# Taking a hand-written scheduler's operations by longest remaining path, and letting PSUM copies choose their engine

## The chip, the core and the metric

The kernel runs on one core of a Trainium2 chip. A core has five instruction streams that work side by side: TensorE (PE in the profile; its weight loads are PEld), VectorE (DVE), ScalarE (ACT), GpSimd (POOL) and SyncE (SP, which here only issues transfers). TensorE writes its products into PSUM, eight banks of 128 partitions by 512 fp32 values; VectorE and ScalarE read them there. The streams wait for each other by semaphores. The metric is the device time of one execution in microseconds, and the median over several runs is compared.

## What is computed

Two layers, each of a linear attention and a gated block, over x of 2048 rows by 512 columns in bf16. The attention has 32 heads of 16 columns. Cut to what matters:

```python
def _A_ref(x, wqkv, w_phi, wo):
    q, k, v = split_heads(x @ wqkv)
    pq, pk = q @ w_phi, k @ w_phi          # per head
    phi_q = concat(softmax(pq), softmax(-pq))
    phi_k = concat(softmax(pk), softmax(-pk))
    kv = phi_k.T @ v                       # summed over all 2048 rows
    z = phi_k.sum(rows)
    o = (phi_q @ kv) / (phi_q @ z + 1e-6)
    return merge_heads(o) @ wo

def _B_ref(x, W_gate, W_up, W_down):       # 512 -> 1376 -> 512
    return (relu(x @ W_gate) * (x @ W_up)) @ W_down

for _ in range(2):
    x = x + _A_ref(_layernorm(x), ...)
    x = x + _B_ref(_layernorm(x), ...)
```

`kv` and `z` need the keys of all rows before the first query can be answered. That is the one barrier in each layer.

## The kernel before

**Scheduler.** The kernel describes itself as a list of `Op` objects and plans its own order while it is built. Each `Op` (line 43) has an engine, a function that emits the instruction, what it reads and writes, and two durations in ns: `occ`, how long it holds its engine, and `lat`, when its result is there. `Program.op` (69) and `Program.dma` (74) append them in program order. `derive` (79) turns reads and writes into dependences. A buffer that is used in turn gives a dependence of the next writer on the last readers, so rings of buffers tie the program's parts together; between two products into the same PSUM bank only the order is kept. `schedule` (117) is a list scheduler: it repeatedly looks at all operations whose predecessors are placed, works out for each the earliest start on its engine, and takes the one with the smallest pair of start and `prio`. `prio` is the index in the program (line 55). So an operation that can start now goes ahead of a more important one that must wait, and among those that can start at the same time the one that stands earlier in the program goes first. A PSUM bank is given out when the first product that writes it is placed, and comes back when its last reader is done. Signals between engines cost 120 ns and within an engine 60 ns in the plan (59 and 60). `plan` (184) then places the semaphore waits, and `emit` (221) writes each engine's operations in the planned order. On the chip each engine goes through its own list in that order, whatever happens.

**Work.** The 2048 rows are 4 blocks (`st`) of 4 tiles (`t`) of 128 rows. x stays in SBUF throughout.

- `fold` (382) multiplies the key and query weights by the per-head `w_phi` once, at the start.
- `layernorm(st)` (401): for each of four tiles `bn_stats` and `bn_aggr` on VectorE; then the reciprocal square root of the four variances together, in twelve small VectorE steps, each waiting for the one before (415 to 423); then for each tile the apply into `ytile` (429; four buffers), four TensorE transposes, and a copy out of PSUM into `yT` (437 to 441): odd tiles on VectorE, even ones on ScalarE.
- `keys(st, b)` (447): for each tile the key and value products, two exponentials on ScalarE into `expk` (six buffers), the sums `Zk` (466; two buffers) and their reciprocals `rZk` on VectorE, a copy of the values into `vsb` on ScalarE (three buffers), and two GpSimd products `vhat` (475). For the block: the `kv` products and a copy or addition into `kvsum` (488, 491) on VectorE.
- `sums()` (494): the barrier. Eight pairs of VectorE steps make `ZDw` (500) and `kvbd` (503) from `kvsum`.
- `queries(st, b)` (507): 16 products and 8 exponentials on ScalarE into `expq`.
- `attend(st)` (516): 32 narrow products `zd`; a chain on VectorE (a copy `Zs` at 530, then `zm`, `zden`, the reciprocal `zr` and `atok`); transposes of `atok` and the copy `aT` (542); then, for each of four column groups, two products that spread `aT` over the partitions, two VectorE products into `expq` (547), the numerator products, and a copy `oT` on ScalarE (552); at last the products with `wo` and the residual additions (561).
- `glu(st, b)` (563): for each of 11 column groups four gate and four up products, a relu on ScalarE (576; `gate_sb` has three buffers) and a product on VectorE into `hT` (578; 22 buffers); then for each tile 11 down products into one bank, and a residual.

**Order.** In the program (602 to 617) the four blocks' layernorms and keys come first. Then, in each layer: `sums`; `out_of_a(0)` (queries, attention and layernorm of block 0); and for each block `st`: `out_of_a(st + 1)`, `glu(st)`, and then `into_a(st)` (the next layer's layernorm and keys) in layer 1, or the four stores of the block in layer 2. Every store writes the one name `R("out")`, so each store depends on the store before it.

Of the kernel before, what the change touches and what calls it, by code (L numbers as in the profile page):

```python
# [42 lines left out]
class Op:  # L43
    __slots__ = ("idx", "eng", "fn", "reads", "writes", "occ", "lat", "name", "is_dma", "nbytes",
                 "deps", "odeps", "users", "missing", "ready", "start", "finish", "cnt", "stream", "prio")

    def __init__(self, idx, eng, fn, reads, writes, occ, lat, name, is_dma=False, nbytes=0):
        self.idx, self.eng, self.fn = idx, eng, fn
        self.reads, self.writes = list(reads), list(writes)
        self.occ, self.lat, self.name = float(occ), float(lat), name  # L50
        self.is_dma, self.nbytes = is_dma, nbytes
        self.deps, self.odeps, self.users = set(), set(), []
        self.missing, self.ready = 0, 0.0
        self.start = self.finish = self.cnt = self.stream = None
        self.prio = idx


class Program:
    SYNC = 120.0
    SAME = 60.0  # L60
# [12 lines left out]

    def dma(self, eng, fn, reads=(), writes=(), nbytes=0, name=""):
        o = Op(len(self.ops), eng, fn, reads, writes, self.DMA_ISSUE[eng], 0, name, True, nbytes)
        self.ops.append(o)
        return o

# [37 lines left out]

    def schedule(self):
        self.derive()
        free = {e: 0.0 for e in ENGINES}
# [3 lines left out]
        left = len(self.ops)  # L123
        for o in self.ops:
            if not o.missing:
                ready[o.eng].append(o)
# [4 lines left out]
        while left:  # L131
            best = None
            for e in ENGINES:
                for o in ready[e]:
                    s = max(free[e], o.ready)
# [7 lines left out]
                    key = (s, o.prio)  # L143
                    if best is None or key < best[:2]:
                        best = (s, o.prio, o)
            assert best is not None, "no operation can go on"
            s, _, o = best
            ready[o.eng].remove(o)
# [10 lines left out]
            o.start = s  # L159
            if o.is_dma:  # L160
                free[o.eng] = s + o.occ
# [3 lines left out]
            else:  # L165
                free[o.eng] = s + o.occ
                o.finish = s + o.lat
            for r in set(o.reads) | set(o.writes):
                if isinstance(r, Bank):
                    r.left -= 1  # L170
                    if not r.left:
                        t = max(x.finish + (0.0 if x.eng == "pe" else self.SYNC) for x in r.ops)
                        banks.append((t, r.bank, r))
            for u in o.users:
                if o.idx in u.deps:
                    t = o.finish + (self.SAME if u.eng == o.eng and not o.is_dma else self.SYNC)
                    u.ready = max(u.ready, t)
                u.missing -= 1
                if not u.missing:
                    ready[u.eng].append(u)  # L180
# [58 lines left out]
def build_kernel(nc, A_x, A_wqkv, A_w_phi, A_wo, W_gate, W_up, W_down, out):  # L239
# [8 lines left out]
    with ExitStack() as ctx:  # L248
# [58 lines left out]
        op, dma = prog.op, prog.dma  # L307
# [4 lines left out]
        def mm(ps, view, lhsT, rhs, start, stop, reads, n, name):  # L312
            lat = 0.4167 * n + 167
            op("pe", lambda e: e.matmul(view(ps), lhsT, rhs, start=start, stop=stop),  # L314
               reads=reads, writes=[ps], occ=max(25.0, 0.4167 * n + 2.6), lat=lat, name=name)

        def tr(ps, view, src, reads, name):
            op("pe", lambda e: e.transpose(view(ps), src, ident[:]),  # L318
               reads=list(reads) + [R("ident")], writes=[ps], occ=56, lat=220, name=name)
# [4 lines left out]
        def b16half(ps):  # L324
            return ps.b16()[:, 0:512]

# [8 lines left out]
        def load_x(t0, t1):  # L335
# [27 lines left out]
           reads=[R("mask8a")], writes=[R("mask8")], occ=150, name="mask8")  # L363
        op("pool", lambda e: e.affine_select(EC[:].rearrange("p g (h j) -> p g h j", j=16), ones[:].rearrange("p (g h j) -> p g h j", g=8, j=16),
                                             [[-8, 8], [-1, 8], [0, 16]], ALU.is_equal, 0.0, base=0, channel_multiplier=1),
# [35 lines left out]
        def layernorm(st):  # L401

            for t in range(4 * st, 4 * st + 4):
                op("dve", (lambda t: lambda e: e.bn_stats(stats[:, t, :], x_sb[:, t, :]))(t), reads=[R("x", t)], writes=[R("st", t)], occ=580, lat=680, name=f"bn{t}")  # L404
                op("dve", (lambda t: lambda e: e.bn_aggr(mv[:, t, :], stats[:, t, :]))(t), reads=[R("st", t)], writes=[R("mv", t)], occ=70, lat=172, name=f"ba{t}")  # L405
            ts = range(4 * st, 4 * st + 4)
            var = mv[:, 4 * st:4 * st + 4, 1:2]
            y = rstd[:, 4 * st:4 * st + 4, :]
            v, hx, t1 = rsv[:, st], rsh[:, st], rst[:, st]
            Rmv, Ry, Rv, Rh, Rt = [R("mv", t) for t in ts], [R("rs", t) for t in ts], [R("rv", st)], [R("rh", st)], [R("rt", st)]  # L410

            def small(fn, reads, writes):
                op("dve", fn, reads=reads, writes=writes, occ=65, lat=160, name="rstd")

            small(lambda e: e.tensor_scalar(v, var, float(EPS_LN), None, op0=ALU.add), Rmv, Rv)
            small(lambda e: e.tensor_scalar(hx, var, 0.5, 0.5 * float(EPS_LN), op0=ALU.mult, op1=ALU.add), Rmv, Rh)
            small(lambda e: e.tensor_single_scalar(t1.bitcast(I32), v.bitcast(I32), 1, ALU.logical_shift_right), Rv, Rt)
            small(lambda e: e.tensor_scalar(y.bitcast(I32), t1.bitcast(I32), -1, 0x5F3759DF, op0=ALU.mult, op1=ALU.add), Rt, Ry)
            for _ in range(2):
                small(lambda e: e.tensor_tensor(t1, y, y, ALU.mult), Ry, Rt)  # L420
                small(lambda e: e.tensor_tensor(t1, t1, hx, ALU.mult), Rt + Rh, Rt)
                small(lambda e: e.tensor_scalar(t1, t1, -1.0, 1.5, op0=ALU.mult, op1=ALU.add), Rt, Rt)
                small(lambda e: e.tensor_tensor(y, y, t1, ALU.mult), Ry + Rt, Ry)
            b = cnt["yT"] % NYT
            cnt["yT"] += 1
            for t in ts:
                yb = cnt["y"] % NY
                cnt["y"] += 1
# [7 lines left out]
                if tt % 2:  # L436
                    op("dve", (lambda ps, dst: lambda e: e.tensor_copy(dst, b16half(ps).rearrange("p (c n) -> p c n", c=NC)))(ps, dst),
                       reads=[ps], writes=[R("yT", b, tt)], occ=328, lat=415, name=f"ycp{t}")
                else:
                    op("act", (lambda ps, dst: lambda e: e.activation(dst, b16half(ps).rearrange("p (c n) -> p c n", c=NC), ACT.Copy))(ps, dst),  # L440
                       reads=[ps], writes=[R("yT", b, tt)], occ=480, lat=600, name=f"ycp{t}")
# [5 lines left out]
        def keys(st, b):  # L447
# [30 lines left out]
            for g0, g1 in ((0, 3), (3, 6), (6, 8)):  # L478
# [8 lines left out]
                if st == 0:  # L487
                    op("dve", (lambda ps, dst, n: lambda e: e.tensor_copy(dst, ps.f32()[:, 0:n]))(ps, dst, n),  # L488
                       reads=[ps], writes=[R("kvs", g0)], occ=490, lat=580, name="kvs")
# [26 lines left out]
        def attend(st):  # L516
# [13 lines left out]
            op("dve", lambda e: e.tensor_copy(Zs[:, g], zdv(zd)[:, :, 0]), reads=[zd], writes=[R("Zs", g)], occ=330, lat=420, name="Zs")  # L530
# [11 lines left out]
            op("dve", lambda e: e.tensor_copy(aT[:, g, :], b16half(pa)), reads=[pa], writes=[R("aT", g)], occ=328, lat=415, name="aT")  # L542
            for c in range(NC):
# [8 lines left out]
                op("act", (lambda c, pn: lambda e: e.activation(oT[:, g, c, :], full(pn), ACT.Copy))(c, pn), reads=[pn], writes=[R("oT", g, c)], occ=480, lat=610, name=f"oT{st}")  # L552
# [49 lines left out]
        for st in range(NS):  # L602
            into_a(st)
# [71 lines left out]
```

## Time and profile before

| what | value |
|---|---|
| median of 3 runs | 454.07 us (452.1 to 454.61) |
| profiled execution | 453.24 us |
| its span, first to last instruction | 451.5 us |
| mean granted TensorE clock | 0.985 |
| HBM read, written | 8.44 MB, 2.10 MB |

The profile's page gives, for one execution, the busy time of each engine and, in 40 slices of the span (11.3 us each), the busy share in tenths: 9 is 90% or more. A view by stretches gives the same for stretches that are asked for, with the share of full speed that TensorE's clock was granted. A group of instructions shows its number, its total busy time, the mean ns of one, and the engine's idle time just ahead of them with what ended it. The timeline lists instructions in order of time; in square brackets stands the idle time of the engine ahead of one, and what it waited for. All matmuls go through the helper at line 314 and all transposes through that at line 318, so they are told apart by their tiles.

### The profile page before, as it was taken

How to read it: one execution, taken by the hardware profiler on the slowest of the kernel's cores; microseconds unless marked ns; L12 is line 12 of the kernel's file. 1: busy time of each engine (PE TensorE's matmuls, PEld its weight loads, DVE VectorE, ACT ScalarE, POOL GpSimd, SP SyncE). 2: the span in 40 equal slices, each digit the busy share in tenths (PEclk: the TensorE clock that was granted, in tenths of full speed). 3: DMA queues.
4: the chain of work that ended last, by engine and by line, in shares of the span. 5: the costliest groups of instructions: out<-in, count | busy, mean ns of one | idle time of the engine just before them, and what ended most of it. 6: DMA issues, size and time to landing. Idle time of an engine off the chain costs nothing.

```text
span 451.5 us, 6587 instructions
## 1 busy us (share of the span) xinstructions
PE 419.7 (93%) x2512; PEld 211.2 (47%) x2560; DVE 331.3 (73%) x819; ACT 182.0 (40%) x329; POOL 72.9 (16%) x75
## 2 busy tenths in 40 slices
PE   3969899789999999999999999887999999999997
PEld 2545556334544544444445444632454454444443
DVE  5999977999669956997578476799963863883342
ACT  4768687223406440453145249622340340341230
POOL 3335780000000700070007005100000000000000
PEclk9999999979999999999999999988999999999999
DMA  8930000000000000000000000000001001000001
GB/s 260 384 107 1 0 1 2 1 0 1 0 1 2 1 1 0 2 0 1 0 1 1 1 0 1 1 1 1 0 2 46 1 0 37 12 1 23 23 1 46
DMA packets 9567, 10.95 MB, mean 24 GB/s; under 512 B 992, under 2 KB 8512, under 8 KB 9536
## 3 DMA queue, kind: packets, MB, share of 16 engines
q1 hardware_dynamic: 7952, 9.47, 6.1%
q10 hardware_dynamic: 1584, 1.07, 0.8%
q8 instruction: 20, 0.33, 0.3%
q14 instruction: 11, 0.09, 0.1%
HBM read 8.44 MB, written 2.10 MB: 23 GB/s over the span
## 4 chain that ended last, share of the span: by engine, by line
PE 77%; DVE 19%; DMA 1%; issue 1%; ACT 1%; POOL 0%; SPq 0%
PE pb L314 74%; DVE expq L547 4%; PE pb L318 3%; DVE stats L404 3%; DVE x_sb L561 2%; DVE Zk L466 1%; DMA x_sb<-in_A_x_dram 1%; DVE kvsum L491 1%; DVE ytile L429 1%; DVE zr L535 1%; DVE hT L578 1%; DVE kvsum L488 1%; DVE kvbd L503 0%; DVE mv L405 0%; DVE Zs L530 0%
## 5 line engine op out<-in xcount | busy, mean ns | idle before, releaser
L576 ACT ACTIVATE gate_sb<-pb 128x512 bf16<-128x512 f32 (+1 forms) x88 | 52.5, 596 | 138.3 <-PE pb L314 136.0
L475 POOL TENSOR_TENSOR vhat<-vsb,rZk 128x544 bf16<-128x544 bf16 x64 | 68.5, 1102 | 210.6 <-DVE rZk L468 195.4
L578 DVE TENSOR_TENSOR hT<-gate_sb,pb 128x512 bf16<-128x512 bf16 (+1 forms) x88 | 59.8, 680 | 44.0 <-PE pb L314 43.8
L314 PE MATMUL pb<-yT,Wg 128*128 128x512 bf16 (+1 forms) x340 | 91.1, 379 | 0.4
L314 PE MATMUL pb<-yT,Wu 128*128 128x512 bf16 (+1 forms) x345 | 91.1, 379 | 0.3
L314 PE MATMUL pb<-Wd,hT 128*128 128x512 bf16 (+1 forms) x344 | 77.0, 379 | 0.4
L561 DVE TENSOR_TENSOR x_sb<-x_sb,pb 128x512 bf16<-128x512 bf16 x64 | 42.2, 683 | 47.0 <-PE pb L314 47.0
L314 PEld LDWEIGHTS pb<-Wd,hT 128*128 128x128 bf16 (+1 forms) x352 | 34.3, 98 | 41.5
L314 PEld LDWEIGHTS pb<-yT,Wu 128*128 128x128 bf16 (+1 forms) x352 | 34.8, 100 | 37.2
L314 PEld LDWEIGHTS pb<-yT,Wg 128*128 128x128 bf16 (+1 forms) x352 | 34.7, 100 | 36.5
L552 ACT ACTIVATE oT<-pb 128x512 bf16<-128x512 f32 x32 | 18.9, 597 | 68.6 <-PE pb L314 68.5
L404 DVE BATCH_NORM_STATS2 stats<-x_sb 128x6 f32<-128x512 bf16 x64 | 42.6, 675 | 1.0 <-DMA x_sb<-in_A_x_dram 0.5
L466 DVE TENSOR_REDUCE Zk<-expk 128x64 f32<-128x1024 bf16 x32 | 37.9, 1190 | 5.4 <-ACT expk L464 5.3
L547 DVE TENSOR_TENSOR expq<-expq,pb 128x512 bf16<-128x512 bf16 x64 | 41.2, 677 | 0.9 <-PE pb L314 0.9
L513 ACT ACTIVATE expq<-pb 128x512 bf16<-128x512 f32 x64 | 33.0, 623 | 18.9 <-PE pb L314 18.8
L464 ACT ACTIVATE expk<-pb 128x512 bf16<-128x512 f32 x64 | 35.0, 602 | 9.6 <-PE pb L314 6.9
L314 PE MATMUL pb<-wo_sb,oT 128*128 128x512 bf16 x125 | 34.4, 379 | 0.3
L314 PE MATMUL pb<-Wkp,yT 128*128 128x512 bf16 x121 | 32.7, 383 | 0.6 <-issue 0.2
L314 PE MATMUL pb<-wv,yT 128*128 128x512 bf16 x126 | 32.7, 379 | 0.1
L314 PE MATMUL pb<-yT,Wqp 128*128 128x512 bf16 x121 | 30.9, 379 | 0.2
L314 PE MATMUL pb<-aT,EC 128*128 128x512 bf16 x64 | 21.7, 460 | 9.6 <-DVE aT L542 9.5
L314 PE MATMUL pb<-vhat,expk 128*128 128x136 bf16 x256 | 25.0, 223 | 3.3 <-POOL vhat L475 2.9
(59 smaller groups left out, 378.0 us busy)
## 6 DMA issues: line engine op xcount, KB each, us to landing
out_dram<-x_sb SPq DMA_DIRECT2D x16, 128.0 KB, 1.7
x_sb<-in_A_x_dram SPq DMA_DIRECT2D x3, 512.0 KB, 10.0
Wg<-in_B_W_gate_dram SPq DMA_DIRECT2D x1, 1376.0 KB, 11.9
Wu<-in_B_W_up_dram SPq DMA_DIRECT2D x1, 1376.0 KB, 12.9
Wd<-in_B_W_down_dram SPq DMA_DIRECT2D x1, 1280.0 KB, 16.1
hT<-in_A_wqkv_dram ACTq DMA_DIRECT2D x1, 512.0 KB, 5.0
x_sb<-in_A_x_dram SPq DMA_DIRECT2D x2, 256.0 KB, 4.7
wv<-in_A_wqkv_dram ACTq DMA_DIRECT2D x1, 512.0 KB, 8.4
```

The source lines that it names most:

```text
L314: op("pe", lambda e: e.matmul(view(ps), lhsT, rhs, start=start, stop=stop), reads=reads, writes=[ps], occ=max(25.0, 0.4167 * n + 2.6), lat ...
L318: op("pe", lambda e: e.transpose(view(ps), src, ident[:]), reads=list(reads) + [R("ident")], writes=[ps], occ=56, lat=220, name=name)
L404: op("dve", (lambda t: lambda e: e.bn_stats(stats[:, t, :], x_sb[:, t, :]))(t), reads=[R("x", t)], writes=[R("st", t)], occ=580, lat=680, ...
L464: op("act", (lambda i, s, pk: lambda e: e.activation(expk[:, i, s, :], full(pk), ACT.Exp, scale=1.0 - 2.0 * s))(i, s, pk), reads=[pk], wri ...
L466: op("dve", (lambda i, zb: lambda e: e.tensor_reduce(Zk[:, zb, :], expk[:, i, :, :].rearrange("p s (h f) -> p (s h) f", f=16), AX.X, ALU.a ...
L475: op("pool", (lambda i, s, vb, rz: lambda e: e.tensor_tensor(vhat[:, i, s, :, :], vsb[:, vb, :, :], rZk[:, rz, s * 32:(s + 1) * 32].unsque ...
L513: op("act", (lambda c, s, ps: lambda e: e.activation(expq[:, st, c, s, :], full(ps), ACT.Exp, scale=1.0 - 2.0 * s))(c, s, ps), reads=[ps], ...
L547: op("dve", (lambda c, sg, ps: lambda e: e.tensor_tensor(expq[:, st, c, sg, :], expq[:, st, c, sg, :], full(ps), ALU.mult))(c, sg, ps), re ...
L552: op("act", (lambda c, pn: lambda e: e.activation(oT[:, g, c, :], full(pn), ACT.Copy))(c, pn), reads=[pn], writes=[R("oT", g, c)], occ=480 ...
L561: op("dve", lambda e: e.tensor_tensor(x_sb[:, t, :], x_sb[:, t, :], full(ps), ALU.add), reads=[R("x", t), ps], writes=[R("x", t)], occ=590 ...
L576: op("act", (lambda m, gb, pg: lambda e: e.activation(gate_sb[0:m, gb, :], pg.f32()[0:m, :], ACT.Relu))(m, gb, pg), reads=[pg], writes=[R( ...
L578: op("dve", (lambda m, gb, hb, pu: lambda e: e.tensor_tensor(hT[0:m, hb, :], gate_sb[0:m, gb, :], pu.f32()[0:m, :], ALU.mult))(m, gb, hb, pu),
```

## The change

The operations and their arithmetic stay the same, but for one term: the halved variance of the layernorm is made from the variance with the epsilon added (`v`), where it was made from the variance itself. What changes is the order in which the scheduler takes the operations, its table of durations, and the engine of some copies.

- `rank` gives every operation the length of the longest way from it to the end of the program, by the planner's durations; `prio` is its negative, so among operations that can start at the same time the one with the longest way goes first. The program's index only breaks ties.
- `SYNC` becomes a table: signals to TensorE cost 90 ns in the plan, from TensorE none, between VectorE and ScalarE 35 or 92, and so on; the latencies of products and transposes are raised.
- `either` makes an operation that can go to one of two engines. When the scheduler takes it, it goes to the engine on which it ends first.
- `copy` uses it for five copies out of PSUM: `yT` (which was split by odd and even tiles), the first block's `kvsum`, `Zs` and `aT` (which were on VectorE), and `oT` (which was on ScalarE).
- `layernorm` reserves its `ytile` buffers ahead of its operations; the sequence of buffers is the same.

```diff
+    SYNC = {("dve", "dve"): 35.0, ("act", "dve"): 35.0, ("act", "act"): 92.0, ("dve", "act"): 92.0,
+            ("dve", "pool"): 80.0, ("act", "pool"): 80.0, ("pool", "pool"): 150.0}
+    SYNC_TO_PE, SYNC_OF_PE, SYNC_ELSE = 90.0, 0.0, 120.0
...
+    def either(self, ways, reads=(), writes=(), name=""):
+        eng = next(iter(ways))
+        o = self.op(eng, ways[eng][0], reads, writes, ways[eng][1], ways[eng][2], name)
+        o.alts = ways
+        return o
...
+    def rank(self):
+        way = [0.0] * len(self.ops)
+        for o in reversed(self.ops):
+            lat = self.DMA_LAT + o.nbytes / self.DMA_BW if o.is_dma else o.lat
+            for u in o.users:
+                step = lat + self.sync(o.eng, u.eng) if o.idx in u.deps else o.occ
+                way[o.idx] = max(way[o.idx], way[u.idx] + step)
+            o.prio = -way[o.idx]
...
-                    key = (s, o.prio)
-                    if best is None or key < best[:2]:
-                        best = (s, o.prio, o)
+                    key = (s, o.prio, o.idx)
+                    if best is None or key < best[:3]:
+                        best = (s, o.prio, o.idx, o, e)
...
+            if o.alts:
+                s, e = min((max(free[x], t) + o.alts[x][2], x) for x in o.alts for y, t in ready[x] if y is o)
+                o.eng = e
+                o.fn, o.occ, o.lat = o.alts[e]
+                s -= o.lat
...
-            lat = 0.4167 * n + 167
             op("pe", lambda e: e.matmul(view(ps), lhsT, rhs, start=start, stop=stop),
-               reads=reads, writes=[ps], occ=max(25.0, 0.4167 * n + 2.6), lat=lat, name=name)
+               reads=reads, writes=[ps], occ=max(25.0, 0.4167 * n + 2.6), lat=max(300.0, 0.4167 * n + 180) if n > 32 else 420, name=name)
...
+        def copy(ps, dst, view, writes, dve, act, name):
+            either({"dve": (lambda e: e.tensor_copy(dst, view(ps)), dve, dve + 88), "act": (lambda e: e.activation(dst, view(ps), ACT.Copy), act, act + 120)},
+                   reads=[ps], writes=writes, name=name)
...
-            small(lambda e: e.tensor_scalar(hx, var, 0.5, 0.5 * float(EPS_LN), op0=ALU.mult, op1=ALU.add), Rmv, Rh)
+            small(lambda e: e.tensor_scalar(hx, v, 0.5, None, op0=ALU.mult), Rv, Rh)
...
-                if tt % 2:
-                    op("dve", (lambda ps, dst: lambda e: e.tensor_copy(dst, b16half(ps).rearrange("p (c n) -> p c n", c=NC)))(ps, dst),
-                       reads=[ps], writes=[R("yT", b, tt)], occ=328, lat=415, name=f"ycp{t}")
-                else:
-                    op("act", (lambda ps, dst: lambda e: e.activation(dst, b16half(ps).rearrange("p (c n) -> p c n", c=NC), ACT.Copy))(ps, dst),
-                       reads=[ps], writes=[R("yT", b, tt)], occ=480, lat=600, name=f"ycp{t}")
+                copy(ps, dst, lambda p: b16half(p).rearrange("p (c n) -> p c n", c=NC), [R("yT", b, tt)], 328, 480, f"ycp{t}")
...
+                    copy(ps, dst, (lambda n: lambda p: p.f32()[:, 0:n])(n), [R("kvs", g0)], 490, 400, "kvs")
...
+            copy(zd, Zs[:, g], lambda p: zdv(p)[:, :, 0], [R("Zs", g)], 330, 270, "Zs")
...
+            copy(pa, aT[:, g, :], b16half, [R("aT", g)], 328, 480, "aT")
...
+                copy(pn, oT[:, g, c, :], full, [R("oT", g, c)], 590, 480, f"oT{st}")
```

## The prediction

> **What bounds the kernel now.** I read the page first (part 1, then the 40 slices), to see which engine is full and when.
>
> ```profile
> span 451.5 us, 6587 instructions
> ...
> PE 419.7 (93%) x2512; PEld 211.2 (47%) x2560; DVE 331.3 (73%) x819; ACT 182.0 (40%) x329; POOL 72.9 (16%) x75
> ...
> PE   3969899789999999999999999887999999999997
> PEld 2545556334544544444445444632454454444443
> DVE  5999977999669956997578476799963863883342
> ACT  4768687223406440453145249622340340341230
> POOL 3335780000000700070007005100000000000000
> ```
>
> TensorE is the bound. It is idle 451.5 - 419.7 = 31.8 us, and the 9s show that nearly all of that lies in slices 0 to 8, 25 to 27 and 39. No order can beat 419.7 us by much, so the change can only win from those 31.8 us, or add to them. Second view: busy time of each engine by stretch (columns: PE, PEld, DVE, ACT, POOL, granted clock, DMA share, GB/s).
>
> ```profile
> 12.00:34.00 22.00, 18.01 (x140) 10.71 (x140) 21.66 (x66) 15.54 (x30) 8.60 (x8) 1.00 0.68 241
> 34.00:72.00 38.00, 36.17 (x267) 20.55 (x271) 33.46 (x74) 29.97 (x58) 25.72 (x24) 1.00 0.00 1
> 72.00:80.00 8.00, 7.11 (x117) 4.63 (x117) 6.73 (x25) 4.98 (x10) 0.00 (x0) 1.00 0.01 3
> 80.00:90.00 10.00, 7.16 (x59) 3.60 (x58) 10.00 (x23) 2.39 (x4) 0.00 (x0) 0.98 0.01 2
> 90.00:101.00 11.00, 8.94 (x30) 3.34 (x32) 10.59 (x35) 2.39 (x4) 0.00 (x0) 0.70 0.00 0
> ...
> 282.00:292.00 10.00, 8.87 (x149) 6.27 (x150) 6.64 (x29) 7.03 (x14) 2.03 (x2) 1.00 0.01 2
> 292.00:303.00 11.00, 9.97 (x68) 4.75 (x69) 10.71 (x27) 2.39 (x4) 0.00 (x0) 0.84 0.01 1
> 303.00:318.00 15.00, 10.74 (x55) 4.62 (x54) 14.59 (x44) 3.58 (x6) 0.00 (x0) 0.89 0.00 1
> ```
>
> TensorE's idle time is 4.0 us in 12 to 34, 1.8 in 34 to 72, 5.8 in 72 to 101, 6.4 in 282 to 318. (The rest: 7.7 before 12 us, loads and the first layernorm; 2.95 at the end, the last residual and its store; 3 us spread over all else.) In 12 to 34, 80 to 101 and 292 to 318 VectorE is 96 to 100% busy: these are the start, and the first attention of each layer, when no gated block is ready to fill TensorE. Third view, the timeline there:
>
> ```profile
> 86.80 0.61 PE L318 MATMUL pb<-ident,atok 128*128 128x128 bf16 x8
> ...
> 91.30 0.39 DVE L542 COPY aT<-pb 128x512 bf16<-128x512 bf16 x1
> ...
> 91.75 3.17 PE L314 MATMUL pb<-aT,EC 128*128 128x512 bf16 x7 [4.34 <-DVE aT L542]
> ```
>
> The copy of aT is ready at 87.4 and runs at 91.3, behind residuals and bn_stats on VectorE, while ScalarE is idle. Last, the groups that price the two homes of a copy:
>
> ```profile
> L440 ACT ACTIVATE yT<-pb 128x512 bf16<-128x512 bf16 x32 | 18.7, 607 | 13.8 <-PE pb L318 13.4
> L437 DVE COPY yT<-pb 128x512 bf16<-128x512 bf16 x32 | 12.6, 413 | 1.5 <-PE pb L318 1.5
> ```
>
> **The change part by part**, against the profiled execution: 453.24 us, a span of 451.5 and 1.74 around it; it lies 0.83 under the median of 454.07.
>
> (a) *Start.* The second layernorm has its first bn_stats at 12.48 and its apply at 32.39. Its own work is 4 bn_stats at 0.59 apart, 4 bn_aggr, 12 small steps 0.2 apart and 1.4 of apply: 6.5 us. The rest are Zk reductions (1.19 each) and rZk (0.54) of the first key tiles, which stand earlier in the program, and bn_stats of later blocks. TensorE starves meanwhile, and GpSimd waits 11.3 us for the next vsb. By the new rank the layernorm goes first: Zk has two buffers, so the planner's chain Zk, rZk, Zk is (1200+35+534+35)/2 = 0.90 us a tile, 14.4 us for sixteen; tile 4's layernorm has twelve tiles of that behind it (10.8) plus its own steps and its keys (some 6.5), 17 us. But rank only chooses between operations that are ready. The small steps stand 195 ns apart in the planner and hold VectorE for 70, so another operation still slips into each gap: 12 x 0.58 = 7 us instead of 13.4 - 2.4 = 11. With the two Zk before it also gone (19.0 becomes 16), the apply comes near 16 + 2.4 + 7 = 25.4 to 28, some 4 to 7 us earlier. TensorE can gain no more than it idles in 12 to 72, 5.8 us, and VectorE's total is unchanged. I take **-3**; bounds -5.8 and +2 (Zk late, so that GpSimd, 16 x 2.15 = 34.4 us, ends last).
>
> (b) *sums().* The eight ZDw steps now go before the eight kvbd (0.2 apart), which only the later num products need. The last ZDw starts at 72.25, with six kvbd between it and the last kvsum: 6 x 0.2 = 1.2 us, while VectorE then waits 1.20 us for the zd products, where the kvbd now fit. **-1 in each layer, -2**; bounds -2.4 and 0.
>
> (c) *Copies.* From 73.8 to 103.4 VectorE is what the first gate product waits for. In it lie four Zs (0.42), three aT (0.39) and two yT copies (0.42): by their spacing on the engine (0.31 to 0.34) 9 x 0.32 = 2.9 us a layer. ScalarE is busy 2.39 of 11 us there, so most leave; where VectorE comes free within 0.18 us the planner keeps an aT. I take two thirds: **-2 a layer, -4**; bounds -6 and +1.2 (three copies of each layer on the path at 607 instead of 413 ns, with nothing gained). A Zs or kvsum copy on ScalarE is in no row: between the 417 ns of VectorE's Zs and the 597 ns of ScalarE's 128x512, and I take the middle; nobody waits long. oT may now go to VectorE (0.68 for 0.60): nothing where ScalarE is idle.
>
> Two rules bear on (c). The Trainium skill, "ScalarE: Activation LUTs", section "Rules for kernel authors", says to use VectorE and not ScalarE for plain elementwise work. The rows agree on the duration (413 against 607) but not on the end: at 87.4 VectorE was 3.9 us away. By the rule alone (c) would be the +1.2. "TensorE: Matmul & The Clock Gate", section "HAM oscillation — how this bites in real kernels", says to leave no TensorE gap over about 3.4 us, since the clock then halves; the row shows such a gap, 4.34 us, and a clock of 0.70 after it. Closing it would by that rule give half of 3.4 us in each layer, an estimate, so -3.4 more in all.
>
> I take **0** for that gap, because VectorE is busy 10.59 of 11 us in the slow stretch and hides it; if that cover were gone it would be worth 11 x 0.30 = 3.3 us a layer, the low side of the range.
>
> (d) *What is put off.* In layer 1 the old order is attention 1, gated block 0, keys 0, attention 2, gated block 1, keys 1 and so on. The ytile buffers (four, one layernorm deep) still force the layernorms into that order. But keys lead only to sums(): tile 0 has 14.4 + 1.6 us of rank above the sums, while every gate product of block 3 has 11.8 for its way through h, down product, residual, layernorm and keys, plus 3.6 for the four key tiles after it. So keys 0 to 2 become filler and mostly run after the gated blocks. Behind those, TensorE then has 128 products 0.216 us apart (four take 1.03, one 0.38; 27.6 us), 128 kv 0.059 apart (13 take 0.93, one 0.22; 7.5 us) and 64 query products (13.8): 49 us; GpSimd 34.4 plus 4.4 of entry (271.1 to 275.5 now); VectorE 16 x 1.65 + 12 x 0.5 and two layernorms of 6.5, 45. It should just fit, and queries left over would fill the next idle stretch. I take **+2**; bounds -3.4 (TensorE's idle time from 101 to 292 gone) and +10 (below).
>
> (e) *Order inside accumulations.* With equal ranks TensorE opens several banks side by side. Four down tiles end now 2.38 apart (125.86, 128.24, 130.62, 133.00), hiding three residuals and bn_stats; ending together they delay the layernorm by 3 x 1.3 = 3.9 us, covered by other blocks' products. At the very end the stores are chained to each other, a rank step of 2.85 us a tile against 11 x 0.216 = 2.38, so the tiles stay in turn and the tail is unchanged. **+1**; bounds 0 and +8.
>
> Planner constants, the reordered slots and hx from v instead of from the variance: the same instructions, **0**.
>
> Sum: -3 - 2 - 4 + 2 + 1 = -6, so 453.2 - 6 = **447 us**.
>
> **Rivals.** *Keys pile up* (the other side). Place: after layer 1's last gated block. For: GpSimd now rests between layer 1's key blocks (35.2 us before the rows at 238.0, 29.0 before those at 275.5), and all its key work would fall into one stretch; at the start twelve tiles took 34.4 to 69, 2.9 us each. Sixteen such are 46 us, behind a layernorm of 6.5 (264.6 to 271.1), 52.5 against 35 of TensorE's own work: +17 where (d) has +2, 462; it decides once query and down products left over are worth less than those 17 us. Against: 13.8 us of queries are there. 20%, 456 to 466.
> *Banks run out.* Side-by-side sums hold up to six of eight banks, and each of 88 gate/up pairs loses 0.1 to 0.2 us: +9 to +18, less 6: 456 to 465. For: the gate ring of three makes equal ranks. Against: VectorE's h takes 0.68 of each pair's 1.73 us. 12%.
> *Little moves.* Dependences fix the order, the gaps still take whatever is ready, (a) to (c) shrink to a microsecond or two: 452 to 455. 11%.
> *More than forecast.* Start closed (-5.8), leftover queries and the clock fill both attention stretches (-6 and more): 433 to 439. 10%.
>
> **How the numbers follow.** The forecast holds 47%, 439 to 451. About 0.5% (2.3 us, what a measurement can tell from no change) around 454.07 gives faster 47 + 10 = 57%, same 11%, slower 20 + 12 = 32%. The range 438 to 460 leaves out some 9% below and 11% above; the forecast's own is 439 to 451.
>
> **What would show it.** Right: the second layernorm's apply before 29 us; aT copies on ScalarE and no 4 us gap before the second set of aT products; the first gate product some 6 us before 103.4; VectorE's busy sum near 320. (d): GpSimd in one block before the layer's end. Wrong: TensorE slices of 7 or 8 between 100 and 290 us, which mean the pile or the banks.

## The result, and the profile after

The changed kernel takes **461.96 us** (median of 4 runs, 461.04 to 462.43) against 454.34 of the kernel before on the same chip: a ratio of 1.0176, 95% interval 1.0154 to 1.0198. It is 1.8% slower where 447 was forecast. The profiled execution has a span of 459.3 us, 7.8 more than before. The page of the changed kernel:

```profile
span 459.3 us, 6610 instructions
...
PE 424.0 (92%) x2560; PEld 211.6 (46%) x2560; DVE 333.7 (73%) x806; ACT 185.4 (40%) x342; POOL 73.5 (16%) x75
...
PE   3876999989999999999989959989999998999897
...
DVE  5999996999557968952982997889743749528443
ACT  4556667554312223343331755755413221440330
POOL 3165573000000000001051568000000000000000
```

The 7 and 6 in slices 2 and 3 are the start; a 5 has appeared at slice 23 (264 to 276 us), in layer 1's last key blocks; two 8s stand late in layer 2 (slices 33 and 37). GpSimd's work of layer 1 has gone into one block, as forecast. TensorE's busy sums can't be set side by side: here all 2560 matmuls are recorded, in the profile of before 48 were missing, and each such gap shows as some 0.1 us of idle time. The view by stretches of the changed kernel (columns as in the prediction; the first two are stretches shown there):

```profile
12.00:34.00 22.00, 18.01 (x118) 10.70 (x119) 21.46 (x59) 12.96 (x25) 8.61 (x8) 0.92 0.69 241
34.00:72.00 38.00, 33.22 (x251) 18.65 (x248) 35.04 (x70) 24.53 (x49) 25.12 (x24) 0.96 0.00 1
...
260.00:280.00 20.00, 15.26 (x114) 9.09 (x114) 18.58 (x33) 10.26 (x21) 13.71 (x14) 0.91 0.00 1
...
420.00:440.00 20.00, 18.20 (x94) 8.36 (x93) 10.81 (x34) 4.78 (x8) 0.00 (x0) 1.00 0.08 27
```

The kernel before, in the last two of these stretches:

```profile
260.00:280.00 20.00, 19.89 (x107) 9.71 (x108) 15.01 (x35) 14.15 (x29) 4.49 (x5) 1.00 0.00 1
...
420.00:440.00 20.00, 19.89 (x92) 9.25 (x93) 8.24 (x12) 6.56 (x11) 0.00 (x0) 1.00 0.02 7
```

From 34 to 72 TensorE idles 4.8 us where it idled 1.8; from 260 to 280 it idles 4.7 where it idled 0.1, at a clock of 0.91; from 420 to 440 it idles 1.8. What happens from 260 to 280 is in the timeline of the changed kernel:

```profile
264.11 4.28 POOL L526 TENSOR_TENSOR vhat<-vsb,rZk 128x544 bf16<-128x544 bf16 x4 [0.77 <-DVE rst L477]
264.43 0.80 DVE L478 TENSOR_TENSOR rst<-rst,rsh 128x4 f32<-128x4 f32 x1
265.26 1.03 DVE L479 TENSOR_SCALAR rst<-rst 128x4 f32<-128x4 f32 x1
266.32 1.02 DVE L480 TENSOR_TENSOR rstd<-rstd,rst 128x4 f32<-128x4 f32 x1
267.38 1.03 DVE L477 TENSOR_TENSOR rst<-rstd 128x4 f32<-128x4 f32 x1
268.44 0.16 DVE L478 TENSOR_TENSOR rst<-rst,rsh 128x4 f32<-128x4 f32 x1
...
269.51 0.61 PE L362 MATMUL pb<-ident,ytile 128*128 128x128 bf16 x4 [4.34 <-DVE ytile L485]
```

These are the small layernorm steps, four numbers in each of 128 partitions. One takes 0.16 us when GpSimd rests. By the trace the four `vhat` products, some 1.06 us apart, end at 265.21, 266.26, 267.32 and 268.38, and the steps at 265.23, 266.29, 267.34 and 268.40: each stands still until the product that runs has ended, and as the next step waits for it, that one falls into the next product. Four steps cost 4.01 us instead of 0.8, and TensorE waits 4.34 us for the apply behind them. The views of single lines (ns: least, median, most; first and last start) show which instructions this strikes. Of the changed kernel:

```profile
L479 DVE TENSOR_SCALAR rst<-rst x32: 97/169/1073, 10.4 to 424.4; 128x4 f32<-128x4 f32 x32
...
L485 DVE TENSOR_SCALAR ytile<-x_sb,mv,rstd x64: 307/407/1191, 13.0 to 426.2; 128x512 bf16<-128x512 bf16 x64
...
L550 DVE SCALAR_TENSOR_TENSOR ZDw<-kvsum,mask x16: 152/159/1136, 71.2 to 290.9; 128x8 bf16<-128x8 f32 x16
...
L469 DVE BATCH_NORM_STATS2 stats<-x_sb x64: 655/676/687, 5.5 to 420.1; 128x6 f32<-128x512 bf16 x64
...
L517 DVE TENSOR_REDUCE Zk<-expk x32: 1202/1208/1221, 18.5 to 280.8; 128x64 f32<-128x1024 bf16 x32
```

And of the kernel before, for the first three of them:

```profile
L422 DVE TENSOR_SCALAR rst<-rst x32: 146/169/208, 10.0 to 400.6; 128x4 f32<-128x4 f32 x32
...
L429 DVE TENSOR_SCALAR ytile<-x_sb,mv,rstd x64: 308/407/1192, 11.2 to 402.0; 128x512 bf16<-128x512 bf16 x64
...
L500 DVE SCALAR_TENSOR_TENSOR ZDw<-kvsum,mask x16: 155/156/167, 69.5 to 287.4; 128x8 bf16<-128x8 f32 x16
```

The medians are the same or nearly so. In the changed kernel the greatest of the small steps, the applies and the `ZDw` steps reach a product's length, while bn_stats and the `Zk` reductions never move (at most 687 and 1221), though 6 and 15 of them start beside a product. The kernel before has long ones too: its applies reach 1192, and another of its small steps (L417) 1025. So I counted the steps of these three kinds that start while a `vhat` product runs, and summed the engine time by which they exceed their usual one. Engine time is here a step's end less its start, or less the end of the instruction before it where that is later; usual are 0.10, 0.335 and 0.08 us, from the same steps with GpSimd at rest. Before it is 17 steps and 6.3 us; after, 31 steps and 19.0 us, 10.3 of it up to barrier 1 and 8.7 between there and barrier 2 (4.0 and 2.3 before). These are called **held** steps below.

To see where the span went I cut it at each layer's barrier (the last `kvsum`) and first gate product. Each cell is the length of the stretch in us, and in brackets the part of it that is not TensorE's own work, with each product placed at the start of its weight load and counted at the plan's duration (for the two kinds that the prediction priced the trace has the same, 0.216 and 0.059). That work is 407.5 us in every kernel, but how much of it falls into a stretch depends on the order. The rows below the first two are experiments that the next section describes; "port known" means that the planner is told of the hold, "in turn" that a sum is finished before the next is opened.

| kernel | to barrier 1 | to first gate | to barrier 2 | to first gate | to the end |
|---|---|---|---|---|---|
| before | 70.7 (18.3) | 32.6 (9.1) | 182.6 (2.2) | 32.3 (10.8) | 133.4 (3.7) |
| after | 75.7 (26.1) | 29.3 (4.1) | 185.8 (9.5) | 28.9 (4.2) | 139.6 (7.9) |
| b3, before with short `vhat` | 68.7 (16.3) | 32.1 (8.6) | 181.0 (0.6) | 32.7 (11.2) | 133.4 (3.7) |
| e3, after with short `vhat` | 72.3 (22.7) | 29.3 (4.1) | 178.5 (2.2) | 29.0 (4.3) | 139.6 (7.9) |
| e4, after with port known | 72.0 (19.5) | 30.1 (7.5) | 185.4 (2.3) | 32.6 (12.1) | 135.2 (6.4) |
| e6, after with sums in turn | 77.3 (27.9) | 29.5 (6.6) | 184.1 (6.1) | 29.7 (5.1) | 136.3 (3.7) |
| e10, e3 with sums in turn | 70.4 (21.0) | 27.7 (4.8) | 178.7 (0.7) | 29.7 (5.1) | 136.3 (3.7) |
| e5, copies alone, port known | 66.5 (14.5) | 32.7 (8.4) | 180.9 (2.0) | 32.5 (8.6) | 132.9 (4.5) |
| e9, rank, port known, in turn | 72.5 (17.6) | 28.9 (8.4) | 183.1 (0.8) | 31.4 (12.2) | 134.3 (3.8) |

Both attention stretches became shorter, by 3.3 and 3.4 us. The start, layer 1's gated blocks and keys, and the end of layer 2 became longer by 5.0, 3.2 and 6.2, of which 2.0 in the last is work moved there.

### The profile page after: what moved, and what is told of

It is laid out like the page before. It is cut to its first block, busy times and chain, and to the rows that moved or that the text cites. A ratio compares the mean times of both kernels' runs of the same rounds, so it can differ in the third digit from the quotient of the medians.

```text
span 459.3 us, 6610 instructions
## 1 busy us (share of the span) xinstructions
PE 424.0 (92%) x2560; PEld 211.6 (46%) x2560; DVE 333.7 (73%) x806; ACT 185.4 (40%) x342; POOL 73.5 (16%) x75
## 3 DMA queue, kind: packets, MB, share of 16 engines
q10 hardware_dynamic: 1584, 1.07, 0.8%
## 4 chain that ended last, share of the span: by engine, by line
PE 67%; DVE 30%; ACT 1%; POOL 1%; issue 1%; POOLq 0%
PE pb L358 64%; DVE stats L469 5%; DVE x_sb L611 5%; DVE Zk L517 3%; DVE ytile L485 3%; DVE expq L597 3%; PE pb L362 3%; DVE hT L628 1%; DVE rZk L519 1%; DVE rstd L480 1%; DVE zr L585 1%; DVE rst L478 1%; DVE rst L479 1%; DVE ZDw L550 1%; ACT expk L515 1%; DVE yT L373 1%
## 5 line engine op out<-in xcount | busy, mean ns | idle before, releaser
L358 PE MATMUL pb<-yT,Wu 128*128 128x512 bf16 (+1 forms) x352 | 107.0, 379 | 0.0
L358 PE MATMUL pb<-yT,Wg 128*128 128x512 bf16 (+1 forms) x352 | 105.4, 379 | 1.6 <-DVE yT L373 0.6
L358 PE MATMUL pb<-Wd,hT 128*128 128x512 bf16 (+1 forms) x352 | 93.4, 379 | 1.4 <-DVE hT L628 1.4
L515 ACT ACTIVATE expk<-pb 128x512 bf16<-128x512 f32 x64 | 33.4, 602 | 17.4 <-PE pb L358 17.2
L469 DVE BATCH_NORM_STATS2 stats<-x_sb 128x6 f32<-128x512 bf16 x64 | 40.2, 677 | 0.0
L358 PE MATMUL pb<-Wkp,yT 128*128 128x512 bf16 x128 | 39.7, 398 | 0.2 <-DVE yT L373 0.2
L373 ACT ACTIVATE yT<-pb 128x512 bf16<-128x512 bf16 x33 | 18.9, 604 | 48.2 <-PE pb L362 48.0
L362 PE MATMUL pb<-ident,ytile 128*128 128x128 bf16 x256 | 24.2, 236 | 15.2 <-DVE ytile L485 14.1
L358 PE MATMUL pb<-wv,yT 128*128 128x512 bf16 x128 | 35.1, 379 | 0.4 <-DVE kvsum L541 0.4
L358 PE MATMUL pb<-yT,Wqp 128*128 128x512 bf16 x128 | 33.9, 380 | 0.0
```

The source lines that it names most:

```text
L362: op("pe", lambda e: e.transpose(view(ps), src, ident[:]), reads=list(reads) + [R("ident")], writes=[ps], occ=56, lat=300, name=name)
L373: either({"dve": (lambda e: e.tensor_copy(dst, view(ps)), dve, dve + 88), "act": (lambda e: e.activation(dst, view(ps), ACT.Copy), act, ac ...
L515: op("act", (lambda i, s, pk: lambda e: e.activation(expk[:, i, s, :], full(pk), ACT.Exp, scale=1.0 - 2.0 * s))(i, s, pk), reads=[pk], wri ...
```

## The experiments

The kernel before ran beside each of the three groups (medians 454.68, 453.5 and 453.52). Ratios are against it, with 95% intervals. These medians differ by 1.2 us, so a difference between kernels of two groups is uncertain by about that; where the text gives one, it gives in brackets what the ratios make of it.

**First: the parts alone, and the product by itself.** e1 has the copies and the table without the rank:

```diff
-        self.rank()
```

> The changed kernel without the rank: operations are taken in program order again, the free choice of engine for the copies and the new table of durations stay. Port theory (VectorE's small layernorm steps, applies and ZDw steps stand still while a GpSimd vhat product runs, and the rank moves them into that time): without the rank they go back to where they were, stretched rows fall from about 31 to about 14, and the time is that of before less what the copies save, 449 to 455. Pile theory (keys put off pile up on GpSimd): the same, 449 to 455, since keys go back to their places. Copy theory (ScalarE's copies are later or in the way): 459 to 464, as the changed kernel.

Measured: 459.12 us, 1.0099 [1.0072, 1.0125]. A miss: program order with the new table and free copies is slower than before too, and its held steps rose from 17 to 25 (10.8 us).

e2 has the rank and the table, with each copy on its old engine:

```diff
-            either({"dve": ..., "act": ...}, ...)
+            on_act = name.startswith("oT") or (name.startswith("ycp") and int(name[3:]) % 2 == 0)
+            if on_act:
+                op("act", ...)
+            else:
+                op("dve", ...)
```

> The changed kernel with the rank and the new table, but each copy on the engine it had before. Port and pile theory: the rank alone brings the loss, 460 to 467, at least as slow as the changed kernel. Copy theory: 452 to 456.

Measured: 469.56, 1.0333 [1.0303, 1.0363], above the expected range, with 39 held steps (19.4 us). So the free copies aren't the loss: with the rank they are worth 469.56 - 461.96 = 7.6 us (7.1).

e3 and b3 keep the order of after and of before and shorten the suspected product, from the seventh key tile on, to 2 of the 32 heads:

```diff
+                nh = 32 if cnt["e"] < NE else 2
...
-e.tensor_tensor(vhat[:, i, s, :, :], vsb[:, vb, :, :], ...
+e.tensor_tensor(vhat[:, i, s, 0:nh, :], vsb[:, vb, 0:nh, :], ...
```

> The changed kernel with the same planned order on every engine, but from the seventh key tile on each vhat product covers 2 heads of 32, so 30 of 32 heads of these keys' values are left out and GpSimd is hardly busy. Port theory: the small steps of the end of layer 1 take their 0.16 us again, the first six tiles still stretch some at the start; the time falls by 8 to 12 us to 450 to 454. Pile theory: GpSimd is no pace-maker any more, so it falls too, but the stretched rows at the start and the end were not the cause: rows of 0.16 without a gain in VectorE's time would show it. Theory of sums side by side (four tiles end together, layernorm late): no change, 460 to 463.

> The kernel before with the same shortening of vhat from the seventh key tile on (30 of 32 heads of these keys' values left out). Port theory: before has few stretched rows (4.4 us of small steps, 1.9 of applies), so it gains 2 to 5 us, 449 to 452, and the changed kernel with short vhat is then no more than 3 us slower than this one. Pile theory: before's keys never wait for GpSimd in layer 1, so it gains under 3 us, 451 to 454, and the same remark holds. If the changed kernel with short vhat stays 6 us or more above this one, the loss lies elsewhere than at GpSimd.

Measured: e3 452.26, 0.9945 [0.992, 0.997]; b3 452.06, 0.9933 [0.9907, 0.9959]. With the long product the change costs 7.6 us, with the short one 0.2: **7.4 of the 7.6 us hang on GpSimd's product.** The intervals of e3 and b3 are 1.1 and 1.2 us either side, so the 0.2 is known to some 1.6. The time of b3 alone can't tell the port theory from the pile theory.

The table shows where the product costs. The bracket grows from before to after by 7.8 us at the start and by 7.3 in the stretch to barrier 2; from b3 to e3 by 6.4 and by 1.6; in the other three stretches the two differences agree within 0.5. So 5.7 us of the cost lie in layer 1's late key blocks. Of the start e3 shows little, since its first six tiles' products are as long as before. The view by stretches of e3, for the stretch where the changed kernel had 15.26 busy and a clock of 0.91:

```profile
260.00:280.00 20.00, 18.83 (x149) 10.93 (x151) 15.78 (x32) 14.13 (x30) 3.11 (x14) 1.00 0.01 1
```

And the timeline of e3, on the same small steps of another layernorm beside two short products:

```profile
44.59 0.46 POOL L527 TENSOR_TENSOR vhat<-vsb,rZk 128x34 bf16<-128x34 bf16 x2 [1.75 <-DVE mv L470]
44.78 0.17 DVE L472 TENSOR_SCALAR rsv<-mv 128x4 f32<-128x4 f32 x1
44.99 0.17 DVE L474 TENSOR_SCALAR rst<-rsv 128x4 int32<-128x4 int32 x1
```

The two products take 0.46 us together, and the steps take 0.17. The same L474 in the changed kernel:

```profile
47.13 1.02 DVE L474 TENSOR_SCALAR rst<-rsv 128x4 int32<-128x4 int32 x1
```

4.5 us of held steps are left in e3, nearly all before 40 us, beside the first six tiles' long products.

**Second: keep the product, and let the planner know.** A shorter product is also less work for GpSimd. So e4 and e5 leave it whole and move only the planned start of a step that would fall into one:

```diff
+        def clear(o, s):
+            if o.eng == "dve" and o.name.startswith(("rstd", "apply", "zdw")):
+                for a, b in vh[-4:]:
+                    if a < s < b:
+                        return b
+            return s
...
-                    s = max(free[e], t)
+                    s = clear(o, max(free[e], t))
...
+            if o.name.startswith("vh") and o.eng == "pool":
+                vh.append((s, s + o.occ))
```

e4 is the changed kernel with this, e5 is e1 with it.

> The changed kernel, and in its plan a small layernorm step, an apply or a ZDw step that would start while a vhat product runs starts at that product's end, so that other operations are taken first. Port theory: stretched rows fall from 31 to under 8 and the time from 462 to 452 to 457; a part of the loss stays if the rank itself costs something. Theory that the rank's order is bad by itself (piled keys, sums side by side): 459 to 463.

> The same knowledge in the plan of the version in program order with free copies and the new table (e1, 459.1). Port theory: 446 to 451, faster than before, since the copies' gain is no longer given back to the port. If the copies or the table cost something by themselves: 456 to 460.

Measured: e4 457.1, 1.0079 [1.006, 1.0097], held time down from 19.0 to 7.1 us; e5 449.05, 0.9909 [0.9883, 0.9935], held time down from 10.8 to 3.9, 10 us faster than e1 and faster than the kernel before. So knowing of the product gives 4.9 (4.4) and 10.1 us (8.6) with all of GpSimd's work in place. Another order can move the time by some microseconds for other reasons, so neither alone would settle it; but both gain, and in both the held time falls by more than half.

e6 is the changed kernel with one more rule: all products into one PSUM bank take the rank of the first, so that a sum is finished before the next is opened:

```diff
+        first = {}
+        for o in self.ops:
+            for r in o.writes:
+                if isinstance(r, Bank) and o.eng == "pe":
+                    o.prio = first.setdefault(r, o.prio)
```

> The changed kernel, but all products into one bank have the rank of the first of them, so an accumulation that has begun is finished before the next of equal rank begins. Theory of sums side by side: four down tiles end 2.4 us apart again and the layernorms behind them start earlier, 455 to 459. Port theory alone: 460 to 464, with as many stretched rows as in the changed kernel.

Measured: 457.52, 1.0082 [1.0055, 1.0108]: 4.4 us less than the changed kernel (4.3), with the held time hardly changed (17.3). What side by side means is seen in the timeline of the changed kernel at a block's end:

```profile
219.28 1.03 PE L358 MATMUL pb<-Wd,hT 128*128 128x512 bf16 x4
...
220.79 1.03 PE L358 MATMUL pb<-Wd,hT 96*128 96x512 bf16 x4
221.21 2.48 DVE L611 TENSOR_TENSOR x_sb<-x_sb,pb 128x512 bf16<-128x512 bf16 x4
...
224.80 2.46 DVE L469 BATCH_NORM_STATS2 stats<-x_sb 128x6 f32<-128x512 bf16 x4
```

The four tiles' sums take the tenth column group in turns of one, then the eleventh, and all four residuals come at once. First to last of a gate sum's four products lie 2.93 us apart on average (0.73 before, 0.63 in e6), of a down sum's eleven 10.99 (2.16 and 6.22). The down sums of layer 1 still end within 0.6 us of each other in e6, since all wait for the same last `hT`; so it isn't through them that e6 gains. The largest part of its gain is at the end of layer 2; by the table it also gains 1.7 us in the stretch to barrier 2 and loses 1.6 at the start. By stretches, the changed kernel:

```profile
380.00:400.00 20.00, 18.46 (x114) 8.48 (x110) 15.35 (x44) 6.53 (x12) 0.00 (x0) 1.00 0.08 27
...
420.00:440.00 20.00, 18.20 (x94) 8.36 (x93) 10.81 (x34) 4.78 (x8) 0.00 (x0) 1.00 0.08 27
```

and e6:

```profile
380.00:400.00 20.00, 20.00 (x137) 10.09 (x136) 14.10 (x41) 6.36 (x13) 0.00 (x0) 1.00 0.08 27
...
420.00:440.00 20.00, 19.91 (x104) 9.28 (x103) 11.10 (x30) 5.37 (x9) 0.00 (x0) 1.00 0.08 27
```

TensorE's 1.54 and 1.80 us of idle time around layer 2's last two layernorms (their applies begin at 387.8 and 425.3) are 0 and 0.09 in e6: 3.25 us, as much as the last stretch became shorter (139.6 to 136.3). Which kind of sum carries it was not tried one by one.

e7 has the table alone: no rank, and copies on their old engines (the edits of e1 and e2 together).

> The changed kernel without the rank and with each copy on its old engine: what is left is the new table of durations (and the reserved slots and hx from v). Port theory: any other order falls into GpSimd's time more than the one of before does, 455 to 460, with stretched rows of 9 us or more. Copy theory (in e1 the copies cost 4.5 us): 453 to 456, as before.

Measured: 458.52, 1.0111 [1.0091, 1.0132], 22 held steps (10.4 us). But for the small edits to the layernorm only the planner's numbers differ from before, and it costs 5 us. In program order the free copies (e1, 459.12, ratio 1.0099) change nothing that can be told from the noise.

**Third: the rest of the theories, and both cures together.** e8 takes the forecast's main rival by itself. It is e4, with layer 1's key work 20 us more urgent:

```diff
+        for o in self.ops[self.barrier:]:
+            if o.name.rstrip("0123456789") in ("k", "v", "ek", "Zk", "rZk", "vcp", "vh", "kv", "kvs"):
+                o.prio -= 20000
```

> As e4 (rank, port known in the plan, 457.1), but all key work of layer 1 gets 20 us more rank, so that it goes ahead of the gated blocks and of attention. Pile theory (keys put off to the end of layer 1 cost the time): 450 to 454. If the piling costs little: 455 to 460.

Measured: 457.75, 1.0087 [1.006, 1.0114], against e4's 457.1. In e8 the `vhat` products of layer 1's first key block begin at 174 us instead of 213 in e4, those of the second at 202 instead of 244; the last two blocks' stay at 259 and 278 (259 and 277). Bringing half of the keys forward gains nothing. With the planner not knowing of the hold it wasn't tried.

e9 is e4 with the sums in turn, e10 is e3 with them:

> As e4 (rank, port known in the plan, 457.1), with the products of one bank taken in turn as in e6. Theory of sums side by side: it costs some 4 us beside the port, as e6 showed (462.0 to 457.5), so 451 to 455. If e6's gain came from another place of the vhat products: 456 to 459.

> As e3 (changed kernel, vhat shortened to 2 of 32 heads from the seventh key tile on; 30 of 32 heads of these values left out; 452.3), with the products of one bank taken in turn. With GpSimd nearly out of play the price of side-by-side sums stands alone: 446 to 449 if it is 4 to 6 us, 451 to 454 if it is nothing.

Measured: e9 452.06, 0.9958 [0.9941, 0.9975]; e10 446.41, 0.9832 [0.979, 0.9874]. In turn is worth 5.0 us (5.5) in the one and 5.8 (5.1) in the other, beside the 4.4 of e6. With the sums in turn and most products short, order and copies bring e10 446.41 against b3's 452.06: **-5.7** (-4.6), with an interval of 1.9 either side for e10 alone.

e11 is e9 with a rank that leans on the program's order:

```diff
-            o.prio = -way[o.idx]
+            o.prio = 200 * o.idx - way[o.idx]
```

> A try at a better version: free copies, port known, products of one bank in turn, and as priority the way left to the end less 200 ns for each place in the program, which is between rank and program order. Port theory with sums in turn: 444 to 449, at least as fast as e5 (449.05). If the rank's share is harmful in itself: 450 to 455.

Measured: **445.71, 0.9831 [0.9795, 0.9867]**, faster than both kernels, with the whole computation. Which of its rules brings how much was not split. The page of e11, and after it its view by stretches:

```profile
span 444.0 us, 6591 instructions
...
PE   3779999799999999999999999979999999999997
...
POOL 4166870000003400340016007000000000000000
```

```profile
34.00:72.00 38.00, 37.09 (x320) 21.75 (x324) 32.43 (x70) 30.92 (x61) 25.75 (x24) 1.00 0.01 2
260.00:280.00 20.00, 19.82 (x149) 10.92 (x151) 14.82 (x45) 17.99 (x36) 8.52 (x8) 1.00 0.00 1
```

No slice between 100 and 290 us is below 9, the held time is 3.1 us, and layer 1's GpSimd work is spread again.

## Why the prediction was wrong

**The step that failed is in (a): the sentence "VectorE's total is unchanged"**; (d)'s "two layernorms of 6.5" rests on the same thing. The forecast treated VectorE and GpSimd as independent: a layernorm step was taken at 0.2 us wherever it was put. The order by rank puts the layernorms of urgent blocks among the `vhat` products, at the start and in layer 1's key blocks, and there a step costs up to a whole product: VectorE's held time went from 6.3 to 19.0 us, and 7.4 of the 7.6 us of loss go when the product is short.

The rule that speaks against this change stands in the Trainium skill, "SBUF — State Buffer", section "🔬 SBUF: two separate sides": VectorE and GpSimd share one pair of ports as a lock; a VectorE instruction with two operands in SBUF, or in a two-port mode, and a GpSimd instruction exclude each other for a whole instruction. The traces agree: the steps shown above end within 0.05 us of a product's end, and none of the lines shown exceeds 1.07 us by much (`ZDw` 1.14, apply 1.19). The prediction didn't weigh it, though the trace of before already held 17 such steps.

**(a), -3.** The way to an earlier apply was right: the second layernorm's applies begin at 26.4 us instead of 32.4, in the forecast 25.4 to 28. But the next layernorm's begin at 41.9 instead of 35.5 and the last one's at 52.4 instead of 44.5, and the barrier came 5.0 us later where 3 earlier was forecast. The bound of +2 named only GpSimd's own end. Not all of the start's loss is settled. In the twelve steps of the third layernorm (30.8 to 41.9 us) only 2.2 us are held time; the rest is other work, mostly `Zk` and `rZk`, that slips in between the steps. The forecast knew of such slipping in, but counted it for the second layernorm alone. With short products from the seventh tile on the start still ends 3.6 us later than b3's (72.3 against 68.7), 1.7 with the sums in turn as well; with the port known (e4) it ends at 72.0 instead of 75.7. So a part of the 5.0 is the hold, and how large a part stays open.

**(b) and (c)**, 1 and 2 us a layer: right in sum, 3.3 and 3.4 measured to the first gate product (layer 1's came at 105.0 all the same, where some 6 us before 103.4 was forecast). But (c)'s reason was only in part it. The copies alone leave the stretch as it was (33.0 and 33.0 us in e1, 32.7 and 32.5 in e5). The rank alone (e2) takes it to 29.0 in layer 1, as short as the changed kernel's; in layer 2 to 31.8, where the changed kernel has 28.9, so there the copies bring 2.9. The 0 for the clock stands: over the whole attention stretch of layer 1 the granted clock was 0.90 before and 1.00 after, but e1 has 1.00 there too and its stretch is no shorter. The copies did come off VectorE in part; `Zs` on ScalarE takes less than both neighbours between which the prediction took the middle (417 and 597). In the groups of the changed kernel:

```profile
L373 ACT ACTIVATE yT<-pb 128x512 bf16<-128x512 bf16 x33 | 18.9, 604 | 48.2 <-PE pb L362 48.0
...
L373 DVE COPY aT<-pb 128x512 bf16<-128x512 bf16 x6 | 2.5, 415 | 0.1
L373 ACT ACTIVATE Zs<-pb 128x256 f32<-128x256 f32 x5 | 1.9, 382 | 10.4 <-PE pb L358 10.3
```

The 4.34 us gap ahead of the second set of `aT` products is gone, though six of the eight `aT` copies stayed on VectorE; and `yT` is split 33 to 31 where it was 32 to 32. What free copies bring depends on the order: 7.6 us with the rank, nothing clear of the noise without. VectorE's busy sum was to come near 320 and is 333.7; less the 19.0 us of held time it is 314.7, where before has 331.3 - 6.3 = 325.0. By this count VectorE was relieved of 10.3 us, and 12.7 of held time came in their place.

**(d)**, +2: layer 1's stretch became 3.2 us longer, near the forecast, and for another reason. GpSimd did go into one block before the layer's end (216 to 288 us). With short products that stretch is 2.5 us shorter than b3's (178.5 against 181.0); with long ones the small steps of the layernorm shown above take from 261.2 to 269.0 us, 7.8 us where 2.4 was counted, and in this stretch the failed step costs most, 5.7 us. *Keys pile up* gave 462, and 461.96 was measured, but its mechanism, GpSimd as the pace-maker of 16 tiles, is not what the runs show (GpSimd is busy only 13.71 of the 20 us from 260 to 280): a right number by luck. That the late block puts more products beside the layernorms may be part of the cause; how much an earlier one would spare, with the planner not knowing of the hold, wasn't tried.

**(e)**, +1: the mechanism was right and its size was not, 4.4 to 5.8. The prediction looked for it in layer 1, at residuals behind four down tiles. By the brackets of e3 and e10 only 1.5 us lie there, and 1.7 at the start; 4.2 lie at the end of layer 2, where no other work was left to cover the layernorms; the attention stretches lose 1.5. *Banks run out* named the side-by-side sums too, but at 9 to 18 us and spread over the gate pairs.

**The whole.** From b3 to e10, from e10 to e3 and from there to the changed kernel the steps are -5.7 for order and copies, +5.8 for the sums and +7.4 for GpSimd's product. That they add up to the measured +7.6 is no test, since the last is what the first two leave; and another way through the kernels gives other shares. The forecast's terms without (e) make -7. That -5.7 is near it is in part luck: to barrier 1 e10 is 1.7 us behind b3 where -3 was forecast, the attention stretches are 4.4 and 3.0 ahead, layer 1's is 2.3 ahead where +2 was forecast, and the end 2.9 behind where nothing was.

**Open.** With the port known and the sums in turn, pure rank (e9) is still 3 us (2.2) behind program order with the port known (e5). The table shows where: up to barrier 1 (17.6 us not TensorE's own against 14.5) and in layer 2's first attention (12.2 against 8.6), where e9 has only 31.4 - 12.2 = 19.2 us of TensorE's work left and e5 23.9. Why the rank uses that work up earlier wasn't tried. Part of it may still be the hold, since e9 has 8.0 us of held time left and e5 3.9. e11, which mixes both orders, has 17.2 and 7.7 there, and 3.1 us held.

## What to carry to other kernels

A planner's order is only as good as its prices, and engines that touch a common resource have no fixed price for an instruction: before judging a new order, list which instructions run beside which, and look at the greatest duration of a line, not its mean. To test such a suspicion keep the order and shorten the suspected instruction in both kernels; then keep the instruction and teach the planner. Where priorities are equal among parts of several sums, finish one sum first.

## What the runs showed of the hardware

- A VectorE instruction on 4 numbers per partition took up to 1.07 us beside a GpSimd product of 128x544 (1.11 us on average), and 0.17 beside two of 128x34 (0.46 us together).
- The hold strikes by kind, not by length: small `tensor_scalar` and `tensor_tensor` steps, the applies (0.41 to 1.19 us) and `ZDw` (0.16 to 1.14) are held; bn_stats (at most 0.687), the `Zk` reductions (at most 1.221) and the reciprocals `rZk` (at most 0.546) aren't, though 6, 15 and 9 of them started beside a product.
- A table of planned signal times and latencies alone moved the time by 5 us (e7), with the same instructions, but for one term of the layernorm, on the same engines in another order.
